# A linear-attention kernel followed by a squared-ReLU feed-forward: the bonus term of the first four units formed by TensorE, w loaded to all partitions, and a new order of all steps

## The chip, the cores and the metric

The kernel runs on one core of a Trainium2 chip. The time is device microseconds from start to end of one execution. The core has five engines with queues of their own, each of which works strictly in order: TensorE (PE; its weight loads are shown apart as PEld), VectorE (DVE), ScalarE (ACT), GpSimd (POOL) and SyncE (SP, which only issues DMA transfers here). ACT and POOL issue DMA transfers too.

## The reference

For each of 4 batches and 8 heads of size 48, with a 48 x 48 state that starts at zero, and then a feed-forward over all 3072 tokens:

```python
for t in range(S):                                   # S = 768
    cur = einsum('bhd,bhe->bhde', u * k[t], v[t])
    y[t] = einsum('bhd,bhde->bhe', r[t], state + cur)
    state = w * state + einsum('bhd,bhe->bhde', k[t], v[t])
x = y of all heads side by side                      # 3072 x 384
h = maximum(x @ w_in, 0)                             # w_in 384 x 2048
out = (h * h) @ w_out                                # w_out 2048 x 384
```

The part of y[t] that comes from cur is (sum over d of r u k) times v[t]: one number for each token and head, multiplied into v. It is called the bonus below.

## The kernel before, in words

The tokens are cut into 24 units of 128 (a batch and a chunk of its time, `UNITS`, L17). Inside a unit the recurrence is worked as matrix products: r and k are scaled by powers of w (steps rh, kh; factors Wt, Wk = exp of a multiple of ln w), transposed, multiplied into a 128 x 128 table of scores for each head (A, in the first four units Ap), masked (Bm, Bp), and multiplied by v (Y). What earlier chunks give comes from the state S0W, which U, S0, ts and S carry on. The y of a unit is copied (xs), transposed (X and xTc, or the DMA transpose xX) and enters the feed-forward: F1 (w_in), re (ReLU), sq (square), F2 (w_out), os and out. For the last unit, Fh, oh and outh do F2 and the output in two halves. The feed-forward takes units singly or in pairs (`GROUPS`): the first two and the last two units singly.

The first four units are *paired* (`PAIRED`, L19): two neighbouring chunks of a batch are loaded by one transfer (lp) whose rows interleave even and odd tokens; TK and TR transpose k and r of a pair, KC and RC copy them from PSUM, and Y of a paired unit adds three things in PSUM: the bonus through an identity product (L428 to L433), the state's part (L437) and the masked scores times v (L440 to L446).

The bonus of a unit takes four steps: P0 (r times k, L344), P1 (times u, L348), du (sum over d, L351) and dv (times v, L356). u lies on all partitions in `ub`: a load to four rows (u, L261) and a shuffle (shu, L276).

w is loaded to one partition (L256), its logarithm is taken there (lw, L270) and TensorE spreads it to 128 partitions by a product with ones (bw, L273). Wk.0, Wk.1, Wt.0 and Wt.1 are written to four banks of PSUM (L290); Wk.2 and Wt.2, for all later units, to SBUF. bc (L303) turns ln w into columns, and WLcol and WLm make of it the factor w^128 that carries the state over a chunk.

Z is an identity product with no use of its result; Z.12 issues three of 512 columns, and n % 4 of 128.

The whole program is a list written out in `ORDER` (L23 to L109), walked once (L595). Each entry is step.unit:engine/buffers, where A, D, G, P and S are ACT, DVE, POOL, TensorE and SyncE, and the numbers behind it say which buffer of a pool, or which of the eight PSUM banks, the step's results take (`HELD`, L112). So the list fixes the order on each engine and each reuse of a buffer; waits are added from the data. V.q and W.q are the loads of the weights w_in and w_out, in four slices each, issued by POOL.

The order on the engines at the start is, on DVE: P0.0, kh.0, kh.1, rh.0, shu, rh.1, P1.1, rh.3, rh.2, kh.2, kh.3, du.0, du.1, four Bp; on TensorE: Z, bw, Z, TK.0, Z.4, TR.0, bc, TR.1, Ap.0.1, TK.1, Ap.0.0, U.1, U.0, Z.5, Ap.1.1, U.2, U.3, Y.0, Y.1, X.0, Ap.1.0, X.1, and then F1 of units 0 and 1; on SP: r, k, v of the first pair, then of the second.

## Time and profile before

| | |
|---|---|
| three runs | 170.42, 175.61, 175.85 us; median 175.61 |
| the profiled execution | 170.48 us |
| its span, first to last instruction | 168.8 us |
| granted TensorE clock | 1.00 |
| ACT busy | 108.2 us, 64% |
| DMA moved | 27.76 MB, mean 165 GB/s |

The profile is of one execution. A line "L506 PE" is line 506 of the kernel on TensorE. In the stretches (windows) each engine's busy time comes in the order PE, PEld, DVE, ACT, POOL, then the granted clock, the DMA share and GB/s. The chain of work that ended last gives start, length and what ran. In the timeline the first two numbers are start and length, and brackets hold idle time and what ended it. In the groups of instructions the numbers behind the bar are total busy us and mean ns of one; behind DMA rows stands the median time from issue to landing.

### The profile page before, as it was taken

To read this page: it belongs to the slowest core of one execution; us is meant where nothing else is said; L and a number is where in the kernel's file an instruction comes from. 1 tells how busy PE (TensorE), PEld (TensorE's weight loads), DVE (VectorE), ACT (ScalarE), POOL (GpSimd) and SP (SyncE) were. 2 spreads that over 40 slices of the span, in tenths; PEclk is the share of its full clock that TensorE was granted. 3 is DMA by queue.
4 is the path that set the end of the run, shared out by engine and by line. 5 is a ranking of instruction groups with operands and counts; after the bars stand their busy time and mean duration, and the time that the engine had idled before them with its cause. 6 is when DMAs were issued, how large, how long until landed. Compare 5 with 4: busy or idle time off the path is not lost.

```text
span 168.8 us, 4617 instructions
## 1 busy us (share of the span) xinstructions
PE 163.2 (97%) x1823; PEld 123.5 (73%) x1823; DVE 131.6 (78%) x248; ACT 108.2 (64%) x203; POOL 94.1 (56%) x115
## 2 busy tenths in 40 slices
...
DMA  5999999994599699995997869985679871251132
GB/s 130 324 239 192 211 223 219 195 195 97 101 207 237 126 182 175 233 211 96 215 200 165 189 138 222 210 164 131 143 184 200 194 85 23 78 161 50 47 116 71
DMA packets 97159, 27.76 MB, mean 165 GB/s; under 512 B 91373, under 2 KB 97138, under 8 KB 97138
## 3 DMA queue, kind: packets, MB, share of 16 engines
...
q0 software_dynamic: 2720, 3.15, 10.7%
...
q14 instruction: 7, 0.06, 0.1%
...
## 4 chain that ended last, share of the span: by engine, by line
PE 89%; DVE 5%; DMA 2%; issue 1%; SPq 0%; ACT 0%; DVEq 0%
PE bank L506 38%; PE bank L534 36%; PE bank L412 3%; DMA ldk<-in_k_dram 2%; PE bank L453 2%; PE bank L451 2%; PE bank L464 2%; PE bank L490 2%; PE bank L548 2%; PE bank L441 1%; DVE rk L338 1%; DVE Bm L393 1%; DVE rk L341 1%; PE bank L399 1%; PE bank L429 1%
## 5 line engine op out<-in xcount | busy, mean ns | idle before, releaser
L506 PE MATMUL bank<-xT,W 128*128 128x256 bf16 (+1 forms) x672 | 69.9, 257 | 0.0
L534 PE MATMUL bank<-W,hq 128*128 128x384 bf16 x368 | 68.2, 326 | 0.0
L506 PEld LDWEIGHTS <-W 128*128 128x128 bf16 x672 | 56.7, 98 | 7.3 <-DVE xT L252 0.2
L516 ACT ACTIVATE hr<-bank 128x512 bf16<-128x512 f32 x69 | 39.9, 595 | 30.3 <-PE bank L506 23.2
L534 PEld LDWEIGHTS <-hq 128*128 128x128 bf16 x368 | 34.0, 98 | 18.4
L523 ACT ACTIVATE hq<-hr 128x512 bf16<-128x512 bf16 x74 | 43.5, 628 | 4.0 <-DVE hr L518 3.1
L420 DVE TENSOR_TENSOR Bm<-bank,maskJT 128x512 bf16<-128x512 f32 x40 | 25.6, 682 | 5.7 <-PE bank L412 5.6
L356 POOL TENSOR_TENSOR dv<-ldv,du 128x384 f32<-128x384 f32 (+1 forms) x19 | 16.1, 852 | 23.0 <-DVE du L351 20.3
L348 POOL TENSOR_TENSOR P<-P,ub 128x384 f32<-128x384 f32 x18 | 19.0, 1054 | 10.9 <-DVE P L344 10.5
L518 DVE TENSOR_SCALAR hr<-bank 128x512 bf16<-128x512 f32 x27 | 18.2, 685 | 8.3 <-PE bank L506 6.8
L344 POOL TENSOR_TENSOR P<-ldr,ldk 128x384 f32<-128x384 f32 x12 | 13.5, 1124 | 4.2 <-DMA ldr<-in_r_dram 2.8
L341 POOL TENSOR_TENSOR rk<-ldr,Wt 128x384 bf16<-128x384 f32 x13 | 14.4, 1119 | 0.0
L476 DVE TENSOR_TENSOR xs<-bank,dv 128x384 bf16<-128x384 f32 x20 | 11.0, 554 | 3.8 <-PE bank L453 3.2
L250 ACT COPY os<-bank 128x384 f32<-128x384 f32 (+1 forms) x15 | 6.9, 467 | 11.0 <-PE bank L534 8.1
L351 DVE TENSOR_REDUCE du<-P 128x8 f32<-128x384 f32 x24 | 12.9, 541 | 0.0
L338 POOL TENSOR_TENSOR rk<-ldk,Wk 128x384 bf16<-128x384 f32 x10 | 10.3, 1033 | 2.9 <-DMA ldk<-in_k_dram 2.9
L344 DVE TENSOR_TENSOR P<-ldr,ldk 128x384 f32<-128x384 f32 x12 | 10.1, 844 | 2.3 <-DMA ldk<-in_k_dram 2.3
L252 DVE COPY os<-bank 128x384 f32<-128x384 f32 (+1 forms) x10 | 5.3, 531 | 7.8 <-PE bank L548 5.8
L485 POOL TENSOR_TENSOR S0W<-ts,WLm 128x384 bf16<-128x384 f32 x8 | 8.3, 1039 | 4.5 <-DVE ts L482 4.5
L525 DVE TENSOR_TENSOR hq<-hr 128x512 bf16<-128x512 bf16 x22 | 10.7, 493 | 0.1
L482 DVE TENSOR_TENSOR ts<-bank,S0W 128x384 f32<-128x384 f32 x16 | 8.7, 550 | 1.2 <-POOL S0W L485 0.7
L453 PE MATMUL bank<-vb,Bm 128*128 128x48 bf16 x160 | 9.4, 183 | 0.0
...
## 6 DMA issues: line engine op xcount, KB each, us to landing
...
W<-in_moe_w_in_dram POOLq DMA_DIRECT2D x4, 384.0 KB, 7.5
W<-in_moe_w_out_dram POOLq DMA_DIRECT2D x4, 384.0 KB, 7.4
...
ldr<-in_r_dram SPq DMA_DIRECT2D x2, 384.0 KB, 4.2
```

Source lines behind the costliest of these rows:

```text
L341: e.tensor_mul(rk[slot[f"rk{i}"]][:, 0, :, 0:D], loaded("r", i), Do.factor("t", i % 2 if i < PAIRED else 2))
L344: e.tensor_mul(P0b[slot[f"P{i}"]], loaded("r", i), loaded("k", i))
L348: e.tensor_mul(t, t, ub)
L351: e.tensor_reduce(dub[slot[f"dv{i}"]], P0b[slot[f"P{i}"]], axis=mybir.AxisListType.X, op=ALU.add)
L356: e.tensor_mul(dv_of(i) if i < PAIRED else dvb[slot[f"dv{i}"]], loaded("v", i), t)
L420: e.tensor_mul(Bmb[slot[f"Bm{i}{h}"]], heads(bank(f"bA{i}{h}"), 128), mask_b)
L453: e.matmul(y[:, hc, D * h : D * (h + 1)], m[h][:, hc, :], vb[:, 2 * hc + h, :], start=(c == 0), stop=True, skip_group_check=True,)
L506: e.matmul(hp[:, fi, :], W1[f // 4][:, c, 256 * (f // 2 % 2) : 256 * (f // 2 % 2 + 1)].rearrange("p (m j) -> p j m", j=2)[:, f % 2, :], xt ...
L516: e.activation(hr, hp, AF.Relu)
L518: e.tensor_scalar_max(hr, hp, 0.0)
L523: e.activation(hq, hr, AF.Square)
L534: e.matmul(bank(f"bO{i}")[:, 0:d_model], hqb[slot[f"hq{g},{f // m}"]][:, at : at + L], W2[q][:, f % 4, :], start=(seen[i] == 1 and f % 4 = ...
```

## The change

For the first four units the bonus is made in another way. P0, P1 and du of these units go. pr multiplies the transposed r and k (copies rT and kT) on DVE; dg is a product of TensorE of that with a column pair uw, which gives the sum over d for each token and head; dc copies it from PSUM on ACT; dv multiplies it into v as before. rT and kT carry the powers of w from Wt and Wk; uw is u times w, which takes back what is left of them. It is made on POOL from columns of u and w that four new small loads bring (uc, wc: 48 partitions x 4 values each). The bonus enters y by a step of its own, Yd, after Y instead of at its head; X and xs follow it.

w is loaded to all 128 partitions; lw takes the logarithm there, and bw and bc go. The four factors Wk.0, Wk.1, Wt.0 and Wt.1 lie in SBUF. WLcol takes ln and exp of the columns of w. `ones` and `wrow` go.

The order is new from end to end. At the start it is, on SP: k, r of the first pair, k of the second, v of the first, r and v of the second; on ACT: w, tab, lw, wc.1, Wk.1, wc.0, Wk.0, Wt.0, Wt.1, WLcol, vb.1, dc.0, Wt.2, vb.0, xs.0, xTc.0; on DVE: kh.1, kh.0, rh.0, rh.1, KC.0, RC.0, pr.1, pr.0, four Bp, S0.0, rh.2, rh.3, kh.3, KC.1, pr.2, pr.3; on POOL: mP.0, uc.1, mP.1, uc.0, V.0, kh.2, uw, V.3, V.1, WLm, dv.1, dv.0, u, mJ, V.2; on TensorE: Z.45, TK.0, Z.5, TR.0, Z.11, Ap.0.0, Ap.0.1, dg.0, Z.20, U.0, U.1, Y.0, Yd.0, Y.1, X.0, Yd.1, TR.1, TK.1, F1.0.0, X.1, F1.0.3, Ap.1.1, Ap.1.0, dg.2, F1.1.3. Over the whole list kh stands on POOL 16 times (10 before), P0 on DVE 6 times (12), P1 on DVE 3 times (6), re on ACT 74 times (69), sq on ACT 77 times (74).

```diff
--- before
+++ after
@@ ORDER @@
-mP.0:G lp.r.0:S/0 lp.k.0:S/0 w:A u:G lp.v.0:S/0 mP.1:G P0.1:G/0 tab:A P0.0:D/1 lw:A Z.12:P/0 bw:P/0 Wk.0:A/1 Wk.1:A/2
-kh.0:D/0 Wt.0:A/3 kh.1:D/1 Wt.1:A/4 rh.0:D/0 vb.0:A/0 shu:D vb.1:A/1 rh.1:D/1 P1.1:D Z.20:P/5 TK.0:P/5 Z.4:P/6
-TR.0:P/6 V.0:G V.3:G KC.0:A/0 lp.r.1:S/1 RC.0:A/1 rh.3:D/2 rh.2:D/3 lp.k.1:S/1 kh.2:D/3 kh.3:D/2 bc:P/7 V.1:G WLcol:A
-P1.0:G du.0:D/0 du.1:D/1 TR.1:P/5 RC.1:A/2 Ap.0.1:P/4/3 Bp.0.1.0:D/0 lp.v.1:S/1 vb.3:A/2 WLm:G P0.2:G/2 Bp.0.1.1:D/1
-TK.1:P/1 KC.1:A/3 vb.2:A/3 Wk.2:A Ap.0.0:P/2/6 Bp.0.0.0:D/2 dv.0:G Bp.0.0.1:D/3 dv.1:G U.1:P/7 U.0:P/5 S0.0:D Z.5:P/4
-Ap.1.1:P/4/3 Wt.2:A ts.1:D/0 U.2:P/1 S0.2:D U.3:P/2 Y.0:P/6 ts.3:D/1 V.2:G Y.1:P/5 xs.0:A/0 X.0:P/0 P1.2:G xs.1:A/1
-xTc.0:D/0 Ap.1.0:P/7/1 W.2:G X.1:P/2 P0.3:G/3 P1.3:G du.2:D/2 dv.2:G F1.0.3:P/6 xTc.1:A/1 F1.1.3:P/5 re.1.3:A/0
-F1.1.0:P/0 F1.0.0:P/2 re.0.3:A/1 re.0.0:A/2 F1.0.1:P/5 re.1.0:A/3 Bp.1.0.1:D/4 Bp.1.1.1:D/5 Bp.1.0.0:D/6 re.0.1:A/4
-sq.0.1:A/0 du.3:D/3 dv.3:G Bp.1.1.0:D/7 F1.1.1:P/6 W.1:G Y.2:P/2 xs.2:A/2 sq.1.3:D/1 re.1.1:A/5 Y.3:P/0 W.3:G
...
+w:A mP.0:G tab:A lw:A wc.1:A uc.1:G mP.1:G Wk.1:A uc.0:G wc.0:A lp.k.0:S/0 kh.1:D/0 V.0:G Wk.0:A kh.0:D/1 Z.45:P/0
+TK.0:P/0 Wt.0:A lp.r.0:S/0 rh.0:D/1 Wt.1:A rh.1:D/0 Z.5:P/1 TR.0:P/1 KC.0:D/0 RC.0:D/1 pr.1:D Z.11:P/2 Ap.0.0:P/2/3
+WLcol:A lp.k.1:S/1 kh.2:G/2 uw:G V.3:G Ap.0.1:P/4/5 V.1:G WLm:G lp.v.0:S/0 vb.1:A/0 pr.0:D dg.0:P/6 dc.0:A dv.1:G/0
+dv.0:G/1 Wt.2:A vb.0:A/1 Z.20:P/7 U.0:P/6 Bp.0.0.1:D/0 U.1:P/7 Bp.0.0.0:D/1 Bp.0.1.1:D/2 Bp.0.1.0:D/3 Y.0:P/0 Yd.0:P
+xs.0:A/0 S0.0:D Y.1:P/1 X.0:P/3 xTc.0:A/0 Yd.1:P xs.1:A/1 u:G lp.r.1:S/1 rh.2:D/2 rh.3:D/3 TR.1:P/2 RC.1:A/2 kh.3:D/3
+TK.1:P/5 KC.1:D/3 pr.2:D pr.3:D F1.0.0:P/4 re.0.0:A/0 lp.v.1:S/1 vb.2:D/2 Wk.2:A X.1:P/0 xTc.1:D/1 F1.0.3:P/6
+re.0.3:A/1 sq.0.0:A/0 vb.3:A/3 Ap.1.1:P/3/1 mJ:G V.2:G Ap.1.0:P/2/5 Bp.1.0.0:D/4 dg.2:P/4 dc.2:A dv.3:G/2 F1.1.3:P/0
+dv.2:G/3 re.1.3:A/2 sq.1.3:A/1 F1.1.0:P/6 U.3:P/2 F1.0.1:P/0 U.2:P/4 Bp.1.1.0:D/5 Bp.1.0.1:D/6 Bp.1.1.1:D/7 Y.2:P/3
+Yd.2:P F1.1.1:P/5 S0.2:D ts.1:D/0 xs.2:A/2 ts.3:D/1 Y.3:P/1 Yd.3:P X.2:P/4 xs.3:A/3 F1.1.2:P/7 re.0.1:A/3 X.3:P/3
+xTc.3:D/0 W.2:G sq.0.1:A/2 sq.0.3:A/3 re.1.2:A/4 F1.0.2:P/2 re.0.2:A/5 xTc.2:D/0 ld.r.4:S/4 rh.4:G/4 W.3:G ld.k.4:S/4
+kh.4:G/4 T.4:P/1 Tc.4:A/4 W.1:G shu:D F1.2.0:P/0 F1.2.5:P/3 F1.2.1:P/7 ld.r.5:S/5 rh.5:D/5 re.2.1:D/0 re.1.0:D/2
...
 HELD = dict(
-    ld=["{0}{1}"], lp=["p{0}{1}"], lW=["ws{0}"], kh=["rk{0}"], rh=["rk{0}"], P0=["P{0}"], du=["dv{0}"], vb=["vb{0}"],
+    ld=["{0}{1}"], lp=["p{0}{1}"], lW=["ws{0}"], kh=["rk{0}"], rh=["rk{0}"], P0=["P{0}"], du=["dv{0}"], dv=["dv{0}"], dg=["bU{0}"], vb=["vb{0}"],
     T=["bT{0}"], Tc=["rkT{0}"], XB=["rkT{0}"], TK=["bTK{0}"], TR=["bTR{0}"], KC=["kT{0}"], RC=["rT{0}"],
-    A=["bA{0}0", "bA{0}1"], Ap=["bA{0}{1}0", "bA{0}{1}1"], Bm=["Bm{0}{1}"], Bp=["Bm{0}{1}{2}"],
+    A=["bA{0}0", "bA{0}1"], Ap=["bAp{0}{1}0", "bAp{0}{1}1"], Bm=["Bm{0}{1}"], Bp=["Bmp{0}{1}{2}"],
     Y=["bY{0}"], xs=["xs{0}"], U=["bU{0}"], ts=["ts{0}"], X=["bX{0}"], xTc=["xT"], xX=["xT"],
     F1=["bH{0},{1}"], re=["hr{0},{1}"], sq=["hq{0},{1}"], F2=["bO{0}"], os=["os{0}"], Z=["bZ"],
-    bw=["bW"], Wk=["WkP{0}"], Wt=["WtP{0}"], bc=["bc"], Fh=["bO{0}{2}"], oh=["os{0}{1}"],
+    Wk=["WkP{0}"], Wt=["WtP{0}"], Fh=["bO{0}{2}"], oh=["os{0}{1}"],
 )
 
 
@@ -190,17 +190,21 @@
     S0W = [const.tile([128, HP, 2 * D], BF16, name=f"S0W_{b}") for b in range(B)]
 
     ub = const.tile([128, H, D], FP32, name="ub")
-    wrow = const.tile([1, H * D], FP32, name="wrow")
-    lrow = const.tile([1, H, 64], FP32, name="lrow")
+    lrow = const.tile([128, H * D], FP32, name="lrow")
     urow = const.tile([128, H * D], FP32, name="urow")
-    ones = const.tile([1, 128], FP32, name="ones")
     wcol = const.tile([128, HP], FP32, name="wcol")
+    ucol = const.tile([128, HP], FP32, name="ucol")
+    wlc = const.tile([128, HP], FP32, name="wlc")
+    uw = const.tile([128, HP, 2], BF16, name="uw")
+    pdb = [const.tile([128, HP, 2, 2, 64], BF16, name=f"pd_{q}") for q in range(PAIRED // 2)]
+    dcb = [const.tile([128, 2, H], FP32, name=f"dc_{q}") for q in range(PAIRED // 2)]
     Wk = const.tile([128, H, D], FP32, name="Wk")
     Wt = const.tile([128, H, D], FP32, name="Wt")
     WLm = const.tile([128, HP, 2 * D], FP32, name="WLm")
-
-    nc.vector.memset(lrow[:, :, D:64], 0.0)
-    nc.vector.memset(ones, 1.0)
+    WF = {("k", 0): const.tile([128, H, D], FP32, name="Wk0"), ("k", 1): const.tile([128, H, D], FP32, name="Wk1"), ("t", 0): const.tile([128, H, D], FP32, name="Wt0"), ("t", 1): const.tile([128, H, D], FP32, name="Wt1")}
+
+    nc.vector.memset(wcol, 1.0)
+    nc.vector.memset(uw, 0.0)
     nc.vector.memset(urow.bitcast(BF16), 0.0)
 
     tcol_i = const.tile([128, 3], mybir.dt.int32, name="tcol_i")
@@ -253,7 +257,7 @@
 
     class Do:
         def w(e):
-            e.dma_start(out=wrow, in_=w.rearrange("h d -> (h d)").rearrange("(a n) -> a n", a=1))
+            e.dma_start(out=lrow, in_=bass.AP(tensor=w.tensor, offset=w.offset, ap=[[0, 128], [1, H * D]]))
 
         def u(e):
 
@@ -267,10 +271,7 @@
             e.preload_act_table_set("natural_log_exp_and_others")
 
         def lw(e):
-            e.activation(lrow[:, :, 0:D], wrow.rearrange("a (h d) -> a h d", h=H), AF.Ln)
-
-        def bw(e):
-            e.matmul(bank("bW")[:, 0 : H * D], ones, lrow[:, :, 0:D], start=True, stop=True)
+            e.activation(lrow, lrow, AF.Ln)
 
         def shu(e):
             e.stream_shuffle(ub.rearrange("p a b -> p (a b)"), urow, [0] * 32)
@@ -286,32 +287,39 @@
                 at_least(maskP[a][64 * c : 64 * c + 64].rearrange("p (b q) -> p b q", b=2), -1 - a, [[1, 2], [2, 64]], -2)
 
         def factor(x, n):
+            if (x, n) in WF:
+                return WF[x, n]
             if n < 2:
                 return bank(f"W{x}P{n}")[:, 0 : H * D].rearrange("p (h d) -> p h d", h=H)
             return {"k": Wk, "t": Wt}[x]
 
         def Wk(e, n):
             o = Do.factor("k", n).rearrange("p a b -> p (a b)")
-            e.activation(o, bank("bW")[:, 0 : H * D], AF.Exp, scale=njcol[:, n : n + 1])
+            e.activation(o, lrow, AF.Exp, scale=njcol[:, n : n + 1])
 
         def Wt(e, n):
             o = Do.factor("t", n).rearrange("p a b -> p (a b)")
-            e.activation(o, bank("bW")[:, 0 : H * D], AF.Exp, scale=tcol[:, n : n + 1])
-
-        def bc(e):
-
-            for hc in range(HP):
-                e.matmul(
-                    bank("bc")[:, hc : hc + 1], pair(lrow.rearrange("p (o a) b -> p o a b", o=1), 0, hc), ones[:, 0:1],
-                    start=True, stop=True, skip_group_check=True,
-                )
+            e.activation(o, lrow, AF.Exp, scale=tcol[:, n : n + 1])
+
+        def wc(e, h):
+            e.dma_start(out=wcol[64 * h : 64 * h + D, :], in_=w.rearrange("(a e) d -> e d a", e=2)[h])
 
         def WLcol(e):
-            e.activation(wcol, bank("bc")[:, 0:HP], AF.Exp, scale=float(L))
+            e.activation(wlc, wcol, AF.Ln)
+            e.activation(wlc, wlc, AF.Exp, scale=float(L))
+
+        def uc(e, h):
+            e.dma_start(out=ucol[64 * h : 64 * h + D, :], in_=u.rearrange("(a e) d -> e d a", e=2)[h])
+
+        def uw(e):
+
+            for h in range(2):
+                rows = slice(64 * h, 64 * h + D)
+                e.tensor_mul(uw[rows, :, h], ucol[rows], wcol[rows])
 
         def WLm(e):
             for h in range(2):
-                col = wcol[64 * h : 64 * h + D, :]
+                col = wlc[64 * h : 64 * h + D, :]
                 e.tensor_copy(
                     WLm[64 * h : 64 * h + D, :, D * h : D * (h + 1)],
                     bass.AP(tensor=col.tensor, offset=col.offset, ap=[list(col.ap[0]), list(col.ap[1]), [0, D]]),
@@ -347,11 +355,32 @@
             t = P0b[slot[f"P{i}"]]
             e.tensor_mul(t, t, ub)
 
+        def paired(x, q):
+            return rkTb[slot[f"{x}{q}"]].rearrange("p x y -> p (x y)").rearrange("p (h c a t) -> p h c a t", h=HP, c=2, a=2)
+
+        def pr(e, i):
+
+            q, c = i // 2, i % 2
+            e.tensor_mul(pdb[q][:, :, :, c], Do.paired("rT", q)[:, :, c], Do.paired("kT", q)[:, :, c])
+
+        def dg(e, i):
+
+            o = bank(f"bU{i}")[:, 2 * D : 2 * D + 2 * H].rearrange("p (a h) -> p a h", a=2)
+            for a in range(2):
+                for hc in range(HP):
+                    e.matmul(
+                        o[:, a, 2 * hc : 2 * hc + 2], pdb[i // 2][:, hc, a].rearrange("p c t -> p (c t)"), uw[:, hc, :],
+                        start=True, stop=True, skip_group_check=True,
+                    )
+
+        def dc(e, i):
+            copy(e, dcb[i // 2], bank(f"bU{i}")[:, 2 * D : 2 * D + 2 * H].rearrange("p (a h) -> p a h", a=2))
+
         def du(e, i):
             e.tensor_reduce(dub[slot[f"dv{i}"]], P0b[slot[f"P{i}"]], axis=mybir.AxisListType.X, op=ALU.add)
 
         def dv(e, i):
-            t = dub[slot[f"dv{i}"]]
+            t = dcb[i // 2][:, i % 2, :] if i < PAIRED else dub[slot[f"dv{i}"]]
             t = bass.AP(tensor=t.tensor, offset=t.offset, ap=[list(t.ap[0]), list(t.ap[1]), [0, D]])
             e.tensor_mul(dv_of(i) if i < PAIRED else dvb[slot[f"dv{i}"]], loaded("v", i), t)
 
@@ -383,14 +412,14 @@
                     for h in range(2):
                         p0 = 64 * h
                         e.matmul(
-                            heads(bank(f"bA{q}{a}{h}"), 128)[64 * c : 64 * c + 64, hc, :],
+                            heads(bank(f"bAp{q}{a}{h}"), 128)[64 * c : 64 * c + 64, hc, :],
                             kT[p0 : p0 + D, hc, c, 64 * a : 64 * a + 64],
                             rT[p0 : p0 + D, hc, c, :],
                             start=True, stop=True, skip_group_check=True,
                         )
 
         def Bp(e, q, a, h):
-            e.tensor_mul(Bmb[slot[f"Bm{q}{a}{h}"]], heads(bank(f"bA{q}{a}{h}"), 128), mask_p[a])
+            e.tensor_mul(Bmb[slot[f"Bmp{q}{a}{h}"]], heads(bank(f"bAp{q}{a}{h}"), 128), mask_p[a])
 
         def T(e, i):
             pt = bank(f"bT{i}").bitcast(BF16).rearrange("p (a b) -> p a b", b=128)
@@ -425,24 +454,18 @@
             if i < PAIRED:
                 q, s = i // 2, i % 2
                 rows = slice(64 * s, 64 * s + 64)
-                for a in range(2):
-                    e.matmul(
-                        y[64 * a : 64 * a + 64], identity[rows, rows],
-                        dv_of(2 * q + a)[rows].rearrange("p (a e) d -> p a (e d)", e=2),
-                        start=True, stop=False, skip_group_check=True,
-                    )
                 rT = rkTb[slot[f"rT{q}"]].rearrange("p x y -> p (x y)").rearrange("p (h c t) -> p h c t", h=HP, c=2)
                 for hc in range(HP):
                     if c > 0:
-                        e.matmul(y[:, hc, :], rT[:, hc, s, :], S0W[b][:, hc, :], start=False, stop=False, skip_group_check=True)
+                        e.matmul(y[:, hc, :], rT[:, hc, s, :], S0W[b][:, hc, :], start=(hc == 0), stop=False, skip_group_check=True)
                 for hc in range(HP):
                     for h in range(2):
                         for a in range(2):
                             e.matmul(
                                 y[:, hc, D * h : D * (h + 1)],
-                                Bmb[slot[f"Bm{q}{a}{h}"]][rows, hc, :],
+                                Bmb[slot[f"Bmp{q}{a}{h}"]][rows, hc, :],
                                 vbb[slot[f"vb{2 * q + a}"]][rows, 2 * hc + h, :],
-                                start=False, stop=True, skip_group_check=True,
+                                start=(c == 0 and (hc, h, a) == (0, 0, 0)), stop=False, skip_group_check=True,
                             )
                 return
             t, m, vb = rkTb[slot[f"rkT{i}"]], [Bmb[slot[f"Bm{i}{h}"]] for h in range(2)], vbb[slot[f"vb{i}"]]
@@ -454,6 +477,17 @@
                         y[:, hc, D * h : D * (h + 1)], m[h][:, hc, :], vb[:, 2 * hc + h, :],
                         start=(c == 0), stop=True, skip_group_check=True,
                     )
+
+        def Yd(e, i):
+
+            y, q, s = heads(bank(f"bY{i}"), 2 * D), i // 2, i % 2
+            rows = slice(64 * s, 64 * s + 64)
+            for a in range(2):
+                e.matmul(
+                    y[64 * a : 64 * a + 64], identity[rows, rows],
+                    dv_of(2 * q + a)[rows].rearrange("p (a e) d -> p a (e d)", e=2),
+                    start=False, stop=True, skip_group_check=True,
+                )
 
         def U(e, i):
             o = heads(bank(f"bU{i}"), 2 * D)
```

152 lines of the change are left out of this document (75 added, 77 removed).

## The prediction

> **What bounds the kernel now.** I read the page (busy shares and slices), then the stretches, then the chain of work that ended last, then the timeline of the first 18 us.
>
> ```profile
> span 168.8 us, 4617 instructions
> PE 163.2 (97%) x1823; PEld 123.5 (73%) x1823; DVE 131.6 (78%) x248; ACT 108.2 (64%) x203; POOL 94.1 (56%) x115
> ...
> DMA  5999999994599699995997869985679871251132
> ```
> ```profile
> 12.00:16.00 4.00, 3.74 (x91) 2.60 (x90) 3.97 (x8) 3.23 (x7) 3.98 (x6) 1.00 1.22 193
> 16.00:20.00 4.00, 4.00 (x86) 3.65 (x85) 3.73 (x8) 2.03 (x5) 3.38 (x4) 1.00 1.23 210
> ...
> 28.00:32.00 4.00, 4.00 (x45) 3.20 (x43) 3.52 (x8) 3.49 (x7) 0.50 (x1) 1.00 1.20 223
> ```
> ```profile
> 1.32 4.21 DMA ldk<-in_k_dram
> ...
> 5.63 0.56 DVE P L344
> 6.18 0.93 DVE rk L338 x2
> ...
> 7.52 0.57 DVE ub L276
> ...
> 8.44 1.14 DVE P L348
> ...
> 11.43 0.92 DVE du L351 x2
> ...
> 14.80 0.35 PE bank L429 x2
> 15.15 0.50 PE bank L441 x16
> ...
> 16.99 0.35 PE bank L385 x16
> 17.33 0.29 PE bank L490 x3
> 17.62 4.12 PE bank L506 x72
> ...
> 26.71 0.45 PE bank L399 x8
> ```
>
> From the stretch at 16 us on, the first engine column (TensorE's busy time) equals the length of the stretch and the granted clock (the 1.00) is full. The chain says the same: a k load until 5.53, DVE until 14.8 us, and from Y.0 (L429, L441) on TensorE alone. DVE's 78% and the rest are no limit there. So the kernel is a front of 14.8 us, then a dense queue of TensorE work, then a tail. A change can save only by starting the queue earlier or shortening it; what leaves the other engines afterwards is worth nothing.
>
> **The change part by part.**
>
> *TensorE work from Y.0 to the end.* The rest of the queue holds the same products: Yd is the identity product that Y had, only later. Five blocks ran in the idle front and now stand behind Y.0: TR.1 and TK.1 (eight transposes each, 0.45 as L399 at 26.71), Ap.1.1 (0.35, L385), U.2 and U.3 (0.60 each below). New behind Y.0 is dg.2: eight products of 128 columns of weights by 2 columns. No row has that shape. Bounds: 0.25 (half of the 16 narrow products of L441, 0.50) and 0.45 (the eight transposes); I take 0.25, since L441's narrow products are nearer. Sum 2 x 0.45 + 0.35 + 2 x 0.60 + 0.25 = 2.7 us. So **Y.0 must start before 14.8 - 2.7 = 12.1 us to gain anything**. The fp32 products L273 and L304, dg.0 and all Z stand in the front, where TensorE waits anyway: zero, as long as Z.45 ends before kh.0 does (else TK.0 is late, as in C below).
>
> *When Y.0 starts.* Durations:
>
> ```profile
> 0.81 0.54 ACTq L256 DMA_DIRECT2D wrow<-in_w_dram  x1
> ...
> 1.98 1.46 PE L565 MATMUL bank<-identity 128*128 128x512 bf16 x3 [1.98 <-POOL identity masks.py:199]
> ...
> 2.67 0.52 ACT L270 ACTIVATE lrow<-wrow 1x384 f32<-1x384 f32 x1
> 2.72 0.75 POOL L261 DMA_DIRECT2D urow<-in_u_dram  x1
> ...
> 3.13 1.15 SPq L326 DMA_DIRECT2D ldr<-in_r_dram  x1
> ...
> 6.00 1.02 ACT L299 ACTIVATE bank<-bank,tcol 128x384 f32<-128x384 f32 x2
> ...
> 8.33 1.06 PE L365 MATMUL bank<-identity,rk 128*128 128x128 bf16 x8
> ...
> 10.56 0.62 PE L365 MATMUL bank<-identity,rk 128*128 128x128 bf16 x8
> ...
> 13.96 0.60 PEld L464 LDWEIGHTS <-rk 64*128 64x128 bf16 x16
> ```
> ```profile
> L393 DVE TENSOR_TENSOR Bm<-bank,maskP 128x512 bf16<-128x512 f32 x8 | 5.0, 678 | 0.0
> L525 DVE TENSOR_TENSOR hq<-hr 128x512 bf16<-128x512 bf16 x22 | 10.7, 493 | 0.1
> L252 DVE COPY rkT<-bank 128x1024 bf16<-128x1024 bf16 x1 | 0.7, 686 | 0.0
> L356 POOL TENSOR_TENSOR dv<-ldv,du 128x384 bf16<-128x384 f32 x4 | 3.3, 830 | 0.8 <-DVE du L351 0.8
> ```
>
> k is now SP's first load and r the second. Issued at 0.81, k lands 4.21 later at 5.0. The w load of 128 rows (128 x 1.5 KB = 196 KB) goes ahead of it; it may cost nothing or, at the 1.15 us that SP takes to push each 393 KB load once DMA is full, up to 0.6. Since 4.21 already held a load ahead of it, I take nothing more; r at 6.1.
> ACT: ln at 3.0 (0.52), then wc.1, Wk.1, wc.0, Wk.0, Wt.0, Wt.1, with 0.54 per issue and 0.5 per exponential: Wk.0 done at 5.6, Wt.0 6.1, Wt.1 6.6.
> DVE: kh.1 5.0 to 5.5, kh.0 to 6.2, rh.0 and rh.1 to 7.3, KC.0 to 8.0 and RC.0 to 8.7 (0.69 each), pr.1 to 9.2 (0.49), pr.0 to 9.7, four Bp of 0.62 in a row to 12.2. Gone from this chain are P0.0, shu, P1.1 and two du: 0.56 + 0.57 + 1.14 + 0.92 = 3.2 us.
> But pr.0 releases a second chain: dg.0 on TensorE (10.1), dc.0 on ACT (10.4), and behind it, in ACT's order, Wt.2 (0.59) and vb.0 (0.52) to 11.5; U.0 and U.1 need vb.0 and stand ahead of Y.0: 11.6 + 1.2 = 12.8. **Y.0 at 12.8**, 2.0 earlier than 14.8; then -2.0 + 2.7 = **+0.7 us**.
> Yd.0 needs dv.1 and dv.0 on POOL, behind uw, V.3, V.1, WLm: about 13.0 against Y.0's end at 13.3, so hidden by 0.3. KC and RC on DVE, dc, and the factors in SBUF cost nothing beyond this; their cover is the front.
>
> *The clock.* Eight transposes took 1.06 at 8.33 and 0.62 at 10.56: TensorE ran at half rate for eight microseconds, though its rows there are nearly unbroken from 1.98. I take 0.62 for TK.0 and TR.0, since Z.45 is one unbroken run. If they stay slow, Z.45 (eleven wide products and a narrow one, three wide ones taking 1.46 at 1.98) ends at about 7.0, TK.0 at 8.1, Z.5 at 8.6, TR.0 at 9.7, and RC.0, pr, dg.0 and Y.0 are 1.7 later. The Trainium skill (TensorE: Matmul & The Clock Gate, What's actually happening) says the full clock comes after about 3.4 us of sustained work; by it TK.0 is fast and the sum stays at +0.7. The trace agrees only in part: it warmed far later, after an interrupted start.
>
> *The small loads.* wc and uc bring columns of w and u, 192 values of 4 bytes each, two on ACT's queue and two on POOL's. uw waits for all four; behind it on POOL stand V.3, V.1, WLm, dv.1, dv.0, and on TensorE dg.0, U.0, U.1, Y.0. WLcol waits for wc and holds ACT's vb.1 and dc.0.
>
> ```profile
> W<-in_moe_w_in_dram POOLq DMA_DIRECT2D x4, 384.0 KB, 7.5
> ...
> urow<-in_u_dram POOLq DMA_DIRECT2D x1, 6.0 KB, 4.1
> ```
> ```profile
> DMA to landing us min/median/max: 5.8/7.5/10.1
> ```
>
> uc.0 goes out at about 4.4 (u went out at 2.72 with 0.75; mP.1 lies between). Landing takes between 4.1 us (the tiny u) and 10.1 (the slowest weight load up to 30 us, the last row; their median is 7.5): 8.5 to 14.5. I take 8.5, nearest in size; then uw runs behind kh.2 and ends at about 9.0, and dg.0 is not held. The Trainium skill (DMA: Bandwidth & Descriptors, Rules for kernel authors) speaks against such loads: a strided last dimension becomes one descriptor per element. That would put the landing toward the later bound; no row here shows a load of that form.
>
> *Weights and the rest.* DMA is full (1.20 and more) until 32 us in both kernels, and the bytes are the same but for w. From Y.0, TensorE runs Y.0, Yd.0, Y.1, X.0, Yd.1, TR.1, TK.1: 0.50 + 0.35 + 0.78 + 0.29 + 0.35 + 0.90 = 3.2, so F1.0.0 starts at 16.0; F1.0.3 follows after 0.69 (4.12 / 6) and X.1 at 17.0 and needs V.3, issued at 9.1, landing 7.5 later at 16.6: hidden by 0.4. V.2, behind dv, u and mJ, goes out at about 15.5 and lands at 23.0; F1.1.2 stands some 8.4 us of products behind F1.0.0, at 24.4: hidden by 1.4. W.2, W.3, W.1 and W.0 go out between POOL's multiplies, which are more than before (kh 16 on POOL instead of 10). Six P0, three P1 and six kh fewer on DVE gain nothing: DVE was not the limit. The tail has the same steps.
>
> **Sum.** Against the profiled execution, 170.48 us (span 168.8 and 1.7 around it): 170.48 + 0.7 = **171.2 us**. The median of the three runs is 175.61, 3.0% above that execution.
>
> **The rivals.**
>
> *A. The small loads hold POOL and TensorE: slower.* If uc.0 takes 7.5 and lands at 11.9, uw ends at 12.2, dg.0 12.6, dc.0 12.9, vb.0 14.0, Y.0 15.2: 2.4 later. V.3, issued at 12.3, lands at 19.8, where F1.0.3 is due at 19.4: 0.4 more for all of TensorE's queue, 171.2 + 2.8 = 174.0. At 10.1 it is 2.6 more, 176.6; between them 175.3. It decides beyond 2% from a landing of 11.8 on. For: DMA share 1.20 to 1.23 throughout. Against: the 6 KB u load took 4.1.
>
> *B. The new order stalls where DMA is full: slower.* W.0 stands behind seven multiplies and three issues of POOL after dv.2. A slice of W2 that lands three us late, as the slowest weight load did beside the median (10.1 - 7.5 = 2.6), stops TensorE outright: 171.2 + 2.6 = 173.8, and with a second such wait 176.4; I take 174.5. For: V.3 and V.2 are hidden by 0.4 and 1.4 only. Against: before, with DMA as full, the chain shows no such wait.
>
> *C. TensorE stays at half clock through TR.0:* 171.2 + 1.7 = 172.9. For: the 1.06 at 8.33.
>
> *D. The front is shorter.* If Wt.2 is done before dc.0 and U takes 0.50, as L441's 16 products do, Bp sets Y.0 at 12.2; with k landing 0.5 us earlier and the exponentials keeping up, 11.7: 171.2 - 1.1 = 170.1. To gain over 2% Y.0 would have to start at 12.1 - 3.4 = 8.7, before even RC.0 is done, so faster by 2% needs something outside this argument.
>
> **How the numbers follow.** Chances: forecast 0.43, A 0.24, B 0.16, C 0.07, D 0.06, outside on the fast side 0.04. 2% of 170.48 is 3.4 us (about what a measurement of this kernel can tell from no change): the bounds are 167.1 and 173.9. Forecast, C and D lie within: 0.56; I add 0.02 for the weak ends of A and B: 0.58. Slower 0.38, faster 0.04. The likeliest case's own range is 170.1 to 172.9. The full range goes down to 169.4 (D, with U.2, U.3 at 0.50, dg.2 at nothing and TR.1, TK.1 half covered: 170.1 - 0.7) and up to 177.0: A and B at their lower prices together make 171.2 + 2.8 + 2.6 = 176.6, and A alone at its dearer bound the same. It leaves out less than 2 in 10.
>
> **What would show it.** Right: Y's first product at about 12.8, F1 starting at about 16, no TensorE idle after it, and a dense queue that ends 0.7 later. Wrong: uw ending after 9.5 with dg waiting on POOL (A); TensorE's weight loads waiting for W or xT between 16 and 45 us (B); eight transposes of 1.06 in TK.0 and TR.0 (C); Y.0 before 12.1 (D). The prediction falls if TensorE's queue behind Y.0 grew by something other than 2.7 us, or if that queue has idle in it.

## The result, and the profile after

| | before | after |
|---|---|---|
| runs | 16: 170.42 to 175.85 us, median 174.22 | 16: 175.93 to 179.62 us, median 178.3 |
| ratio of times | | 1.0369, 95% interval [1.0311, 1.0426]: slower |
| the profiled execution: time, span | 170.48, 168.8 us | 179.62, 177.6 us |
| Y.0 starts | 14.80 | 15.71 |
| first product of F1 starts | 17.50 | 22.02 |
| from there to the end | 151.3 | 155.6 |

The forecast was 171.2 us with a range to 177.0. The profiled execution is one of the longer ones (mean clock 0.971); the four shortest, at 0.99, have spans of 173.9 to 174.4, and the ratio leaves the longest runs of both kernels out.

Below, "F1" with a time is the start of F1's first product. "Half clock" means that like products take nearly twice as long as elsewhere: eight transposes 1.06 us, where they take 0.62 at "warm" clock.

Lines of the changed kernel's page, then its stretches (columns as before), then the first stretch of the kernel before:

```profile
span 177.6 us, 4632 instructions
...
PE 166.3 (94%) x1842; PEld 126.7 (71%) x1842; DVE 128.2 (72%) x235; ACT 105.6 (59%) x204; POOL 103.2 (58%) x126
...
PEclk9969669999999999999999999999999999999999
DMA  2999998995999599865897598998777973340022
```
```profile
0.00:4.00 4.00, 2.02 (x5) 0.73 (x6) 2.29 (x13) 1.28 (x1) 2.86 (x15) 1.00 0.15 38
4.00:8.00 4.00, 2.08 (x8) 0.75 (x6) 0.85 (x2) 2.08 (x5) 1.71 (x4) 1.00 1.03 242
8.00:12.00 4.00, 3.76 (x43) 2.75 (x47) 3.25 (x7) 0.57 (x2) 0.00 (x0) 0.57 1.16 249
12.00:16.00 4.00, 2.44 (x67) 1.61 (x57) 2.49 (x5) 2.01 (x6) 3.48 (x7) 1.00 1.14 280
16.00:20.00 4.00, 2.15 (x40) 1.63 (x34) 2.86 (x4) 0.49 (x2) 3.82 (x7) 0.84 1.15 186
20.00:24.00 4.00, 4.00 (x37) 3.67 (x37) 1.63 (x4) 2.39 (x4) 0.00 (x0) 0.50 1.25 219
...
80.00:100.00 20.00, 19.49 (x203) 14.91 (x201) 17.57 (x33) 16.15 (x31) 13.20 (x14) 1.00 0.78 143
```
```profile
0.00:4.00 4.00, 2.02 (x4) 0.78 (x5) 2.34 (x13) 1.80 (x2) 2.87 (x15) 1.00 0.48 120
```

and F1's first row in the timeline of the kernel before (the chain, in the prediction, puts it at 17.62):

```profile
17.50 2.68 PE L506 MATMUL bank<-xT,W 128*128 128x128 bf16 x44
```

Three things stand out. In the first four microseconds the loads move 38 GB/s at a share of 0.15, where before they moved 120 at 0.48. TensorE is idle for four to five tenths of three stretches behind the first (4 to 8, 12 to 16 and 16 to 20 us). And from 20 to 24 us, where it is busy all the time, its clock is 0.50.

The timeline of the changed kernel shows the chain of waits (in brackets, the idle time before and what ended it):

```profile
1.93 3.93 SPq L334 DMA_DIRECT2D ldk<-in_k_dram  x1
...
1.98 4.11 PE L599 MATMUL bank<-identity 128*128 128x512 bf16 x12 [1.98 <-POOL identity masks.py:199]
...
5.88 0.52 ACT L274 ACTIVATE lrow<-lrow 128x384 f32<-128x384 f32 x1 [3.33 <-DMA lrow<-in_w_dram]
...
6.44 0.35 ACTq L305 DMA_DIRECT2D wcol<-in_w_dram  x1
...
7.15 1.03 DVE L346 TENSOR_TENSOR rk<-ldk,Wk 128x384 bf16<-128x384 f32 x2 [3.83 <-ACT Wk L298]
...
8.24 0.86 PE L394 MATMUL bank<-identity,rk 128*128 128x128 bf16 x8 [2.15 <-DVE rk L346]
...
9.42 1.06 PE L394 MATMUL bank<-identity,rk 128*128 128x128 bf16 x8
...
12.06 0.21 ACT L308 ACTIVATE wlc<-wcol 128x4 f32<-128x4 f32 x1 [3.49 <-DMA wcol<-in_w_dram]
...
12.35 0.99 POOL L346 TENSOR_TENSOR rk<-ldk,Wk 128x384 bf16<-128x384 f32 x1 [6.59 <-ACT wlc L308]
...
13.31 0.47 POOL L318 TENSOR_TENSOR uw<-ucol,wcol 48x4 bf16<-48x4 f32 x2
13.71 1.58 POOL L340 DMA_DIRECT2D W<-in_moe_w_in_dram  x2
13.84 0.34 PE L371 MATMUL bank<-uw,pd 128*128 128x2 bf16 x8 [1.49 <-POOL uw L318]
...
15.35 0.72 POOL L323 COPY WLm<-wlc 48x192 f32<-48x192 f32 x2
...
16.15 1.93 POOL L385 TENSOR_TENSOR dv<-ldv,dc 128x384 bf16<-128x384 f32 x2
...
18.13 0.35 PE L486 MATMUL bank<-dv,identity 64*64 64x384 bf16 x2 [1.85 <-POOL dv L385]
...
22.02 1.49 PE L540 MATMUL bank<-xT,W 128*128 128x128 bf16 x12
```

w reaches the 128 partitions at 5.88 (forecast: 3.0), k is multiplied at 7.15 (5.0), the last column of w is in at 12.06 (the forecast had the last small load at 8.5), uw ends at 13.78 (9.0), Yd.0 runs at 18.13 (13) and F1 at 22.02 (16.0). Twelve products of F1 then take 1.49 us, where before 44 took 2.68. kh.2, ahead of uw on POOL, starts at 12.35; its k load, issued at 1.93, lands 10.2 us later, at 12.1, so the releaser that its row names is not the whole story.

### The profile page after: what moved, and what is told of

The parts are those of the page before. It is cut to its first block, busy times and chain, and to the rows that moved or that the text cites. A ratio compares the mean times of both kernels' runs of the same rounds, so it can differ in the third digit from the quotient of the medians.

```text
span 177.6 us, 4632 instructions
## 1 busy us (share of the span) xinstructions
PE 166.3 (94%) x1842; PEld 126.7 (71%) x1842; DVE 128.2 (72%) x235; ACT 105.6 (59%) x204; POOL 103.2 (58%) x126
## 4 chain that ended last, share of the span: by engine, by line
PE 84%; DVE 7%; DMA 4%; POOL 2%; issue 2%; ACT 1%; DVEq 0%
PE bank L540 35%; PE bank L568 30%; DMA ldk<-in_k_dram 4%; PE bank L441 3%; PE bank L476 2%; PE bank L498 2%; PE bank L394 2%; PE bank L474 2%; DVE Bm L449 2%; PE bank L524 2%; PE bank L582 1%; POOL dv L385 1%; DVE rk L346 1%; PE bank L599 1%; PE bank L464 1%
## 5 line engine op out<-in xcount | busy, mean ns | idle before, releaser
L568 PE MATMUL bank<-W,hq 128*128 128x384 bf16 x368 | 66.4, 326 | 0.0
L540 PEld LDWEIGHTS <-W 128*128 128x128 bf16 x672 | 58.3, 100 | 6.8 <-issue 0.2
L550 ACT ACTIVATE hr<-bank 128x512 bf16<-128x512 f32 x74 | 42.0, 597 | 29.4 <-PE bank L540 28.7
L557 ACT ACTIVATE hq<-hr 128x512 bf16<-128x512 bf16 x77 | 45.9, 630 | 4.8 <-DVE hr L552 4.3
L346 POOL TENSOR_TENSOR rk<-ldk,Wk 128x384 bf16<-128x384 f32 x16 | 17.9, 1127 | 6.6 <-ACT wlc L308 6.6
L552 DVE TENSOR_SCALAR hr<-bank 128x512 bf16<-128x512 f32 x22 | 14.9, 685 | 5.6 <-PE bank L540 5.4
L352 POOL TENSOR_TENSOR P<-ldr,ldk 128x384 f32<-128x384 f32 x14 | 14.8, 1058 | 4.8 <-DMA ldk<-in_k_dram 2.5
L385 POOL TENSOR_TENSOR dv<-ldv,du 128x384 f32<-128x384 f32 x13 | 11.0, 848 | 9.8 <-DVE du L380 9.3
L380 DVE TENSOR_REDUCE du<-P 128x8 f32<-128x384 f32 x20 | 10.8, 541 | 0.0
L599 PE MATMUL bank<-identity 128*128 128x512 bf16 (+1 forms) x24 | 7.5, 469 | 2.0 <-POOL identity masks.py:199 2.0
L346 DVE TENSOR_TENSOR rk<-ldk,Wk 128x384 bf16<-128x384 f32 x8 | 6.1, 768 | 3.9 <-ACT Wk L298 3.8
(78 smaller groups left out, 177.6 us busy)
```

Of the source, the lines that this page charges most:

```text
L346: e.tensor_mul(rk[slot[f"rk{i}"]][:, 1, :, 0:D], loaded("k", i), Do.factor("k", i % 2 if i < PAIRED else 2))
L352: e.tensor_mul(P0b[slot[f"P{i}"]], loaded("r", i), loaded("k", i))
L385: e.tensor_mul(dv_of(i) if i < PAIRED else dvb[slot[f"dv{i}"]], loaded("v", i), t)
L540: e.matmul(hp[:, fi, :], W1[f // 4][:, c, 256 * (f // 2 % 2) : 256 * (f // 2 % 2 + 1)].rearrange("p (m j) -> p j m", j=2)[:, f % 2, :], xt ...
L550: e.activation(hr, hp, AF.Relu)
L552: e.tensor_scalar_max(hr, hp, 0.0)
```

## The experiments

The theory to be tested: the front is late since w's load to 128 partitions holds the DMA engines and the small loads hold POOL, ACT and TensorE; TensorE's idle gaps then cost it the clock; and behind Y.0 stands the 2.7 us of work that the prediction counted. Rivals are named with each run. Kernels e are the changed kernel edited, kernels b the kernel before. "Rest" is the span less the start of F1. Starts and landings come from one profiled execution of each kernel.

**What 128 reads of one row do.** In the kernel before, beside its own load, one more load whose result nobody uses: the row of w to all partitions (b1), or 128 different rows, as many bytes (b2).

```diff
+            e.dma_start(out=wide, in_=bass.AP(tensor=w.tensor, offset=w.offset, ap=[[0, 128], [1, H * D]]))          # b1
+            e.dma_start(out=wide, in_=bass.AP(tensor=v.tensor, offset=v.offset, ap=[[H * D, 128], [1, H * D]]))      # b2
```

> The kernel before, with one more load that nothing uses, on ACT's queue right behind the small w load: the 1.5 KB of w to each of 128 partitions. Theory W1 (128 reads of the same 1.5 KB hold up the DMA engines, whatever else is in flight): the DMA share of 0 to 4 us falls from 0.48 to about 0.2, the k load lands at 7 or later instead of 5.5, and the time grows by 1.5 to 2.5 us. Rival W2: it is only 196 KB more, 0.6 us.

> The same with 128 different rows of 1.5 KB (the head of v, 196 KB in one piece) in place of the one row of w. Theory W1: the k load lands at about 6.1, the share of 0 to 4 us stays near 0.48. Rival W2: as late as with the one row.

The landing of that load and the first P0, which waits for r and k, in b1 and then in b2:

```profile
DMA to landing us min/median/max: 5.2/5.2/5.2
```
```profile
7.84 0.56 DVE L346 TENSOR_TENSOR P<-ldr,ldk 128x384 f32<-128x384 f32 x1 [4.52 <-DMA ldk<-in_k_dram]
```
```profile
DMA to landing us min/median/max: 3.4/3.4/3.4
```
```profile
6.03 0.56 DVE L346 TENSOR_TENSOR P<-ldr,ldk 128x384 f32<-128x384 f32 x1 [2.71 <-DMA ldk<-in_k_dram]
```

P0 stood at 5.63 before (its row is in the prediction): the same row costs the loads beside it 2.2 us, the same bytes from 128 rows 0.4. So it is not the bytes. Nor is it the number of packets: in the first 8 us the queue moved 146 of them, 0.20 MB, in both, but they took twice the time with the one row (14.8% of 16 engines' time against 6.7%). The times (178.1 and 176.29, one run each) tell nothing more: in both, later transposes stayed at 1.03 us to the eight, so half clock is in both.

**The small loads beside the others.** b3 issues the four small loads in the kernel before, unused.

```diff
-mP.0:G lp.r.0:S/0
+mP.0:G uc.1:G lp.r.0:S/0
...
-mP.1:G P0.1:G/0
+mP.1:G uc.0:G P0.1:G/0
...
-lw:A Z.12:P/0
+lw:A wc.1:A wc.0:A Z.12:P/0
```

> The kernel before with the four loads of 192 values of 4 bytes, unused, two on ACT behind ln w and two on POOL around the masks. Theory S3 (loads of single values hold DMA): k, r and v land 1 us or more later and the time grows by 1 to 2 us. Rival: 768 values are little against 1024 rows of 384 bytes for each load; the k load stays at 5.5 to 5.8 and the time within 0.5 us of 170.5. Their own landing, 5 to 6 us in full DMA, is the cost in either case.

P0 starts at 5.56 (5.63 without them), and they land 3.4 to 4.2 us after their issue at 2.2 to 5: they harm no other load. The one time, 175.56, has the half clock in it.

**w to four rows.** e1 loads w to four partitions and spreads it by a shuffle on DVE, as the kernel does with u.

```diff
-            e.dma_start(out=lrow, in_=bass.AP(tensor=w.tensor, offset=w.offset, ap=[[0, 128], [1, H * D]]))
+            rows = wrow[:, :]
+            e.dma_start(
+                out=bass.AP(tensor=rows.tensor, offset=rows.offset, ap=[[32 * rows.ap[0][0], 4], [1, H * D]]),
+                in_=bass.AP(tensor=w.tensor, offset=w.offset, ap=[[0, 4], [1, H * D]]),
+            )
+
+        def shw(e):
+            e.stream_shuffle(lrow, wrow, [0] * 32)
```

> The changed kernel with one part undone: w goes to four rows and a shuffle on DVE spreads it, instead of 128 reads of one 1.5 KB row. Theory W (the 128 reads of one row hold up the DMA engines until 5.9 us, and the first k load behind them): w in lrow by about 4.2, k lands at about 5.0 to 5.5 instead of 7.0, kh.1 starts 1 to 1.5 us earlier than 7.15, and the time falls by 1 to 2 us, to about 174 to 175. Rival theory S (the four small loads, and POOL behind them, set the start): kh.1 is earlier but dg.0 is not, and the time stays at 176.

175.09 to 178.31 in four runs, ratio 1.0323 [1.0219, 1.0426]: a gain in time that the spread covers. F1 19.29, rest 153.9. The first four microseconds move 122 GB/s again, and the second k load lands 5.0 us after issue, not 10.2, so kh.2 on POOL no longer waits for it:

```profile
7.49 1.30 POOL L355 TENSOR_TENSOR rk<-ldk,Wk 128x384 bf16<-128x384 f32 x1 [1.74 <-ACT Wk L307]
```

But wcol still lands at 11.94 and dg.0 runs at 12.62: the small loads now hold the front.

**Without the small loads.** e2 leaves them out and takes constants for the columns, so the bonus of the first units and the factor that carries the state are made of other numbers.

```diff
-... lw:A wc.1:A uc.1:G mP.1:G Wk.1:A uc.0:G wc.0:A lp.k.0:S/0 ...
+... lw:A mP.1:G Wk.1:A lp.k.0:S/0 ...
```

> The changed kernel without the four loads of 4-byte values; wcol and ucol are filled with constants, so that the factor of the state and the bonus use constants instead of w and u. Theory S: dg.0 leaves at about 11.5 instead of 13.84, WLm is done earlier, the start of F1 moves 2 us forward, about 174. Theory W: uw still stands behind kh.2 on POOL, which waits for the second k load (landed at 12.1); dg.0 moves by 0.5 at most and the time stays within 0.5 us of 176.

177.98 to 179.03, ratio 1.0458 [1.0389, 1.0527]; F1 21.07. uw runs at 12.36 all the same, behind kh.2, whose k load came late with w wide. Taking away one of two waits that end together brings 0.95 at F1 against the changed kernel's profiled execution, and nothing that the times show.

**The weights first.** e4 issues V.3 and V.1 ahead of kh.2, and uw too; e6 (on e5, below) puts V.3 beside V.0, and uw, WLm and dv ahead of kh.2 and V.1.

```diff
-WLcol:A lp.k.1:S/1 kh.2:G/2 uw:G V.3:G Ap.0.1:P/4/5 V.1:G WLm:G
+WLcol:A lp.k.1:S/1 V.3:G V.1:G uw:G kh.2:G/2 Ap.0.1:P/4/5 WLm:G
```

> The changed kernel with POOL's order changed: V.3 and V.1 are issued right behind V.0, where POOL sits idle (5.8 to 12.3 us), and uw stands ahead of kh.2. Theory P (POOL's order costs the wait of Yd.0: 1.85 us, TensorE idle until dv.0 at 18.1): Yd.0 at about 16, the time 1.5 to 2 us less, about 174. Rival: the two weight loads of 768 KB take DMA from the second k and r loads, k lands later than 12.1, and the time stays or grows by up to 1 us.

> The version with more Z (clock held, 175.9 to 176.5) with POOL's order changed: V.3 right behind V.0, then uw, WLm, dv.1, dv.0, and only then kh.2 and V.1. Theory P2 (uw stands behind kh.2, which waits for the second k load until 11.8, and dv behind the two weight issues and WLm): Yd.0 starts at about 15.5 instead of 17.7 and the time falls by about 2 us, to 174. Rival: uw is held by the columns of w all the same (landed at 12.0), and V.3 takes DMA from the loads of k and r, as the early V.3 and V.1 did in the earlier run: no gain, or slower by up to 2 us.

e4 took 180.47 to 182.44 (1.0633 [1.0546, 1.0719]), e6 177.67 to 181.65 (1.0485 [1.04, 1.057]). The rival was right that it costs, in both, but not in how much, and in e4 not in the load: the second k load lands 9.8 us after issue there, no later than in the changed kernel. In both chains of waits stands the first v load, which the weights overtake; it lands at 17.1 in e4 and 15.1 in e6, where vb.1, its first reader, ran at 13.18 in the changed kernel:

```profile
5.63 11.50 DMA ldv<-in_v_dram
```
```profile
5.68 9.41 DMA ldv<-in_v_dram
```

**More filler for TensorE.** e5 is the changed kernel with Z.77 for Z.45, Z.24 ahead of dg.0 and Z.28 ahead of Yd.0.

> The changed kernel with idle TensorE time filled: Z.77 instead of Z.45 at the start, Z.24 ahead of dg.0 and Z.28 ahead of Yd.0. Theory C (TensorE lost its clock in the idle stretches, 0.57 in 8 to 12 us and 0.50 in 20 to 24): the granted clock stays at 1.0 from 8 us on, F1 starts at about 21 at full rate, and the time falls by 2 to 3 us, to about 173 to 174. Rival: the clock is only a sign, the loads set the pace: no more than 0.5 us less, or some tenths more because the products stand in the way.

175.94, 176.18, 176.24, 176.45: ratio 1.0327 [1.0253, 1.0401]. The spread shrinks from 3.7 us in sixteen runs to 0.5 in four, so the changed kernel's spread is, as far as four runs tell, the clock; the level is that of its best runs, so the clock is only part of the loss. F1 20.22, rest 153.9. From here on the front can be compared at one clock, where the filler holds it. Its chain of waits begins with the second k load, issued by SP at 1.93:

```profile
1.93 9.83 DMA ldk<-in_k_dram
```

**The small loads first, with that filler.** e7 issues them right behind w.

```diff
-w:A mP.0:G tab:A lw:A wc.1:A uc.1:G mP.1:G Wk.1:A uc.0:G wc.0:A lp.k.0:S/0
+w:A wc.1:A wc.0:A uc.1:G uc.0:G mP.0:G tab:A lw:A mP.1:G Wk.1:A lp.k.0:S/0
```

> The version with more Z (175.9 to 176.5) with the four small loads issued first: wc.1 and wc.0 right behind w on ACT, uc.1 and uc.0 ahead of the masks on POOL. Theory S2 (their landing at 12.0 sets uw): uw at about 9, F1 about 2 us earlier, 174. Theory P2: uw stands behind kh.2 and the second k load (11.8), so not more than 0.5 us is gained; and the first k may land some tenths later.

175.15 to 175.54, ratio 1.0287 [1.0268, 1.0305]; F1 19.25, rest 154.1. A gain of 1.0 at F1: kh.2 still waits for its k load, and uw with it. Beside w wide the small loads took 5.4 to 6.5 us though issued first.

**All repairs together.** e8 has e5's filler, w to four rows, the small loads first, e6's order of POOL, and vb.0 ahead of dc.0. e9 is e8 with Z.53, Z.8 ahead of U.0, and neither of the two that e5 added further on.

> All of it together: w by four rows and a shuffle, the small loads first, POOL's order with kh.2 and V.1 behind dv, vb.0 ahead of dc.0 on ACT, more Z. If the front is what the change lost, F1 starts at 16.5 to 17.5 instead of 20.4 and the time is 172 to 173.5. If the order from F1 on costs something of its own beyond the 2.7 us of products that were moved behind Y.0, the time stays at 174 or above with the same start of F1. In no theory is it under the kernel before (170.3 at its best).

> All of it together as before, but with the Z cut to what the loads leave idle (Z.53 at the start, none ahead of dg.0 and Yd.0, Z.8 ahead of U.0), since TensorE's chain ran through them. Y.0 at about 13.1, set by Bp, F1 at about 16.3 instead of 19.1, and the time 2 to 3 us less than 174.6: 171.7 to 172.6. If so, the front can be made shorter than in the kernel before (F1 there at 17.5) and the time is still longer, by the products moved behind Y.0 and the idle of the new order: the term +2.7 of the prediction stands. Rival: the clock falls again without these Z, and the runs scatter up to 176.

e8: 174.54 to 174.98 (1.025 [1.0231, 1.0268]), F1 18.93, rest 154.2; here the filler itself was in TensorE's way, as e9 shows. e9: 173.53 to 174.67 (1.0215 [1.0172, 1.0258]); Y.0's run of products starts at 13.24 and F1 at 16.53, near the forecast, but with less filler the clock fell, in the stretch and in the row of F1:

```profile
16.00:20.00 4.00, 4.00 (x67) 3.83 (x64) 1.99 (x5) 2.53 (x5) 0.85 (x2) 0.59 1.18 193
```
```profile
16.53 1.49 PE L549 MATMUL bank<-xT,W 128*128 128x128 bf16 x12
```

**The clock held, and one repair taken back at a time.** e10 is e9 with Z.69, Z.12 and a Z.13 ahead of Y.0. From it, e11 takes back the four rows, e12 the place of the small loads, e13 the order of POOL (V.3 and V.1 at their old places too).

```diff
-WLcol:A lp.k.1:S/1 uw:G Ap.0.1:P/4/5 WLm:G ...
+WLcol:A lp.k.1:S/1 kh.2:G/2 uw:G V.3:G Ap.0.1:P/4/5 V.1:G WLm:G ...          # e13
```

> The kernel with all three repairs of the front (e9) with three more runs of Z where TensorE stood idle (Z.69, Z.12 and a new Z.13 ahead of Y.0). Account theory (what stays of the loss is work moved behind Y.0 and idle of the new order, all else is front and clock): F1 starts at 16.1 to 16.5, 1.1 to 1.5 ahead of before (17.62), its groups of twelve take 0.69 and not 1.28, the span is 168.8 - 1.3 + 2.7 = 170.2, the time 171.5 to 172.3. If the clock was not what held e9, the time stays at 173.5 to 174.7.

> The kernel before it with one repair taken back: w goes to 128 partitions by one load again. Theory: w lands 0.5 to 1.2 later and k up to 2.5 later; Y.0 and F1 start 1 to 2 later. Rival, that the load's place in the front is covered by the order of POOL and ACT: F1 within 0.3 of the kernel with all repairs.

> All repairs but the place of the four small loads, which stand behind lw again. Theory: the last lands at about 11 to 12, uw and WLcol wait for it, dg.0 at 12 to 13 and F1 1.5 to 2.5 later. Rival (they don't matter by themselves, as when they were taken away): F1 within 0.3.

> All repairs but POOL's order, which is that of the changed kernel: kh.2, uw, V.3, V.1, WLm, then dv. Theory: uw waits behind kh.2 for the second k load, which lands at 11 to 12; dv ends at 16 to 17.5 and F1 starts 2.5 to 3.5 later. Rival, that the second k load now lands early since w no longer holds the DMA engines: F1 within 0.5.

| | us | ratio | F1 | span | rest |
|---|---|---|---|---|---|
| e10 | 172.95 to 173.87 | 1.0137 [1.0063, 1.0212] | 17.17 | 171.1 | 153.9 |
| e11, w wide | 179.83 to 180.52 | 1.0533 [1.0462, 1.0603] | 23.17 | 178.3 | 155.1 |
| e12, small loads late | 175.04 to 179.19 | 1.0248 [1.0149, 1.0347] | 19.86 | 173.8 | 153.9 |
| e13, POOL as changed | 173.51 to 173.78 | 1.0149 [1.0101, 1.0197] | 17.68 | 171.9 | 154.2 |

e12 shows the small loads' own wait, on ACT, POOL and TensorE:

```profile
12.34 0.21 ACT L317 ACTIVATE wlc<-wcol 128x4 f32<-128x4 f32 x1 [4.20 <-DMA wcol<-in_w_dram]
```
```profile
12.50 0.47 POOL L327 TENSOR_TENSOR uw<-ucol,wcol 48x4 bf16<-48x4 f32 x2 [5.98 <-DMA wcol<-in_w_dram]
...
13.83 1.61 POOL L394 TENSOR_TENSOR dv<-ldv,dc 128x384 bf16<-128x384 f32 x2
```
```profile
13.02 0.35 PE L380 MATMUL bank<-uw,pd 128*128 128x2 bf16 x8 [2.39 <-POOL uw L327]
```

The columns of w, issued at 5.5 to 6.0, land 5.4 to 6.3 later; the four small loads issued first, in e10, 4.0 to 4.2 later, hidden. e13 refutes what I expected of POOL's order: its k load now lands at 7.5 and uw is not held.

```profile
7.53 1.01 POOL L355 TENSOR_TENSOR rk<-ldk,Wk 128x384 bf16<-128x384 f32 x1 [1.59 <-DMA ldk<-in_k_dram]
8.50 0.98 POOL L327 TENSOR_TENSOR uw<-ucol,wcol 48x4 bf16<-48x4 f32 x2
```

So that order costs 0.5 us once w is out of the way; kh.2's long wait in the changed kernel was w's doing, as in e1. e11 costs 6.0 at F1, more than expected: with V.3 early as well, v lands at 14.6 (the chain of waits has the load), and TensorE idles and stays at half clock.

```profile
5.41 9.20 DMA ldv<-in_v_dram
```
```profile
12.00:16.00 4.00, 0.81 (x9) 0.42 (x8) 1.79 (x3) 1.37 (x4) 0.25 (x1) 0.91 1.17 299
16.00:20.00 4.00, 4.00 (x44) 2.25 (x43) 2.92 (x4) 0.61 (x2) 4.00 (x5) 0.50 0.97 194
```

**A free bank.** e10 missed its expectation at F1 (17.17, not 16.1 to 16.5): Z.13 shared a bank with Ap and waited for Bp. e14 gives it another bank (P/1 for P/4).

```profile
13.36 0.86 PE L608 MATMUL bank<-identity 128*128 128x512 bf16 x4 [0.74 <-DVE Bm L431]
```

> The kernel with all repairs and the clock held (e10), where Z.13 waited 0.74 us for Bp since its bank was Ap's and so stood 0.8 in front of Y.0; now it takes a free bank. Account theory: Y.0 at 13.3, F1 at 16.4, 1.2 ahead of before; span 168.8 - 1.2 + 2.7 = 170.3, the time 171.6 to 172.4, still no faster than before. If the account is wrong and Y.0 is not what the end hangs on, the time stays at 173.2.

172.02 to 173.01, ratio 1.0112 [1.0087, 1.0137]. Y.0 moved to 13.24, but F1 only to 16.92, since the transposes behind it waited 0.23 us for rh and took 1.43 instead of 1.07:

```profile
15.66 1.43 PE L403 MATMUL bank<-identity,rk 128*128 128x128 bf16 x16 [0.23 <-DVE rk L358]
```

Rest 154.1. No version with the new bonus and order is faster than the kernel before. And even with every repair the chain of waits begins with w, now in four rows, whose load goes out only behind the memset of its tile and lands at 4.99; the k load of 0.81 is in by then (e10):

```profile
1.37 3.62 DMA wrow<-in_w_dram
```

**The kernel before with more filler.** b4 has Z.16, Z.8 and Z.9 for its Z.12, Z.4 and Z.5.

> The kernel before with some more Z in its front (Z.16, Z.8 and Z.9 instead of Z.12, Z.4 and Z.5). Theory C (the spread of the runs, 170.3 to 176.8, is TensorE's clock missing its rise in the interrupted front): all runs lie within 1 us, near 170.5. Rival: the spread has another cause, and runs of 174 to 176 stay among them.

Ratio 1.0014 [1.0, 1.0028]. Eleven of twelve runs lie in 170.38 to 171.2 and one took 176.74; of the seventeen of the kernel before beside it, seven took 174.41 or more. So the filler took most of that spread away, as far as twelve runs tell, but not all, and the expectation that every run would lie within 1 us failed by that one. At its best clock the front of the kernel before doesn't wait for TensorE, so filler there neither costs nor gains.

## Why the prediction was wrong

*The step that failed is "When Y.0 starts"*, in two of its terms, and with them the clock.

"I take nothing more" for the w load. I priced 196 KB by its bytes, at most 0.6 us. It landed 5.1 us after issue, SP's third issue stood 3.93 us, the first k load came at 7.05 for 5.0 and the second at 12.1. Shown by b1 against b2 (2.2 against 0.4 us) and by e1 and e11. Nor did "ln at 3.0" have a price for this load: the row at 2.67 was of a load to one partition, and ln ran at 5.88. The row that I had, 1.15 us for each 393 KB load, was of loads whose rows differ.

"I take 8.5, nearest in size" for the small loads was worked out for uc.0, and uc.0 did land at 8.69 (4.3 us after 4.39). But uw and WLcol needed the columns of w too, and for these the sum has no landing. They stand behind ln w on ACT, so the late w put wc.0 off to 6.44, and it took 5.5 us more: 12.0. That has the effect of rival A by another load: dg.0 waited for uw, which had kh.2 with its late k load ahead of it as well. e12 gives the price of the place alone, 2.7 us at F1, the half clock that follows the wait included. The Trainium skill (DMA: Bandwidth & Descriptors, Rules for kernel authors) states one descriptor for each element of such a load, which I had put toward the later bound. No run here has the same values in another form, so none shows a price of the form: issued early and without w wide, the loads took 3.4 to 4.2 us (b3, e10), as the 6 KB load of u did (4.1); behind full loads 5.4 to 6.3 (e12).

What made F1 late in the changed kernel is Yd.0, which the prediction had "hidden by 0.3", more than Y.0. Y.0 starts 2.9 late (15.71 for 12.8). But uw ended 4.8 late (13.78 for 9.0), V.3, V.1, WLm and dv followed it on POOL in 4.3 us (4.0 in the forecast), and Yd.0 ran 4.8 late (18.13 for 13.3, Y.0's end in the forecast). From there to F1 it took 3.9 where the forecast had 2.7, much of it at half clock: 4.8 and 1.2 are the 6.0 of F1.

The two terms hide each other. With e5's filler F1 starts at 20.22 with both loads as changed and at 19.25 with the small loads alone repaired (e7); with w alone repaired, and the changed kernel's own filler, at 19.29 (e1). With e10's filler and all repaired it starts at 17.17, and taking back the small loads alone costs 2.7 (e12), w alone 6.0 (e11). The fillers differ and are worth up to 1.8 at F1 (e8 against e10), so these prices don't add up.

*The clock: "I take 0.62 for TK.0 and TR.0, since Z.45 is one unbroken run".* Z.45 ended at 6.1 and TensorE idled until 8.24; TK.0 took 0.86, TR.0 1.06 at 9.42, and two more gaps followed. Rival C saw the row but not the cause, a gap behind Z while k and Wk were late, nor its size: the filler of e5 moves F1 by 1.8 us, and the rest falls from 155.6 to 153.9, 1.7 more, against the profiled execution. The Trainium skill (TensorE: Matmul & The Clock Gate, What's actually happening) asks for about 3.4 us of sustained work; the runs agree that an unbroken Z does it (e10: 5.7 us of Z from 1.99, and TK.0 takes 0.62).

```profile
7.96 0.62 PE L403 MATMUL bank<-identity,rk 128*128 128x128 bf16 x8 [0.27 <-DVE rk L355]
```

*"TensorE work from Y.0 to the end", +2.7 us, stood.* From Y.0 to the end it is 157.0 to 157.2 us in e10, e12 and e13, where Y.0 starts at 14.15, 16.84 and 14.66, against 154.0 before (168.8 - 14.80): 3.0 to 3.2 more, with 0.7 of idle in it (157.8 in e14, where the transposes behind Y.0 wait and take longer). The work alone is then about 2.3 to 2.5, and the idle was put at nothing. Counted from F1, in the eight kernels whose first twelve products of F1 are at warm clock (0.83 us: e1, e5, e7, e8, e10, e12, e13, e14), the rest is 153.9 to 154.2 us, whatever the front, against 151.3 before. By the forecast's own numbers it would have been 153.5 (168.8 + 0.7 - 16.0), about half a microsecond less. e10's stretches, and TensorE's longest wait in them:

```profile
20.00:44.00 24.00, 23.82 (x301) 18.95 (x299) 18.36 (x34) 19.13 (x37) 19.61 (x22) 1.00 1.14 198
44.00:80.00 36.00, 35.49 (x390) 27.13 (x388) 31.14 (x53) 23.21 (x45) 22.67 (x24) 1.00 0.91 173
```
```profile
74.48 0.34 PE L533 MATMUL bank<-identity,xs 128*128 128x128 bf16 x3 [0.51 <-DVE xs L519]
```

There TensorE idles 0.18 + 0.51 us, mostly for xs on DVE (in the changed kernel the same wait lies in the stretch from 80 us on, shown above); the kernel before is busy through both stretches. Rival B, a stall on weights, did not happen: no wait of TensorE for a load of W stands in either trace. The prediction's condition for a gain, a start of Y.0 before 12.1 us, was not met even in e14, where it starts at 13.24 with every wait repaired that I could repair.

The sum, for the profiled execution against the forecast: F1 6.0 later (22.02 - 16.0), 1.6 of cold clock behind it (155.6 - 154.0) and 0.5 of idle (154.0 - 153.5) make 8.1; measured 179.62 - 171.2 = 8.4, of which 0.3 lies outside the span (2.0 around it, not 1.7). The changed kernel's shortest run, 175.93, is as long as e5 at warm clock; there 4.7 us remain over the forecast, nearly all of it F1 (4.2 later, 20.22 - 16.0) and idle (0.4, 153.9 - 153.5).

What stays open: how the 1.8 us at F1 between the changed kernel and e5 divides among its three gaps, why w to 128 partitions costs more in e11 than in the changed kernel beyond the late v, and why many reads of one row are slow. No run keeps w's old way (one partition, spread by TensorE) in the new order, so whether the front could have become shorter with it is not shown.
